# Last chunk's feed-forward first, bias rows in DRAM, held and split loads, two blocks normalized on chip, pooled score banks and order rules per stretch, in a fused layernorm, attention and feed-forward kernel

## The chip, the cores and the metric

One core of one Trainium2 chip. The metric is the device time of one execution in microseconds (us). Most executions of one kernel agree within 0.3%, but some runs of the kernel before come 4 to 6 us later with a lower mean granted clock of TensorE (0.987 to 0.991 for 0.996 to 1.0), so the clock of each run is looked at before its time is used.

The engines are called as the profile calls them: PE is TensorE (matrix products), PEld its weight loads, ACT is ScalarE, DVE is VectorE, POOL is GpSimd, SP is SyncE, which only issues transfers. An L with a number is a line of the kernel's own source, so the same work has another line number in the other kernel.

## The reference, cut to what matters

```python
# S = 2048 rows, D = 640, H = 32 heads of Dh = 20, F = 1536; all inputs bf16
def _A_ref(x, wq, wk, wv, wo):                    # one k and one v for all 32 heads
    q = (x @ wq).reshape(B, S, H, Dh).transpose(0, 2, 1, 3)
    k = x @ wk
    v = x @ wv
    scores = jnp.einsum("bhqd,bkd->bhqk", q, k) * (Dh ** -0.5)
    p = softmax(scores)
    o = jnp.einsum("bhqk,bkd->bhqd", p, v)
    return o.transpose(0, 2, 1, 3).reshape(B, S, H * Dh) @ wo

def _B_ref(x, w1, b1, w2, b2):
    h = x @ w1 + b1
    r = where(h > 0, h, 0)
    return (r * r) @ w2 + b2

xn = _layernorm(x)
return x + _A_ref(xn, wq, wk, wv, wo) + _B_ref(xn, w1, b1, w2, b2)
```

## The kernel before

The program is straight-line code whose order is decided when it is built. A list scheduler inside the kernel's source keeps a small model of the engines, and at every step puts the most urgent instruction that could start next onto its engine. On the chip each engine then runs its list in that order, whatever the real times are.

The attention has 32 blocks: 4 chunks of 512 queries by 8 groups of 4 heads. A block has 16 key tiles by 4 heads, so there are 2048 score tiles of 128 keys by 512 queries, each one bank of the on-chip accumulation memory (PSUM) wide. Most tiles become exponentials on ACT, two banks in one activation (a "step"). The others come in "sets" of four heads of one key tile: DVE turns four score banks into 16-bit patterns of approximate exponentials (line L972 of before), and three more passes on DVE or POOL refine them. PE makes the scores as row-tiled products (20 rows of one head each), and everything else as column-tiled products in groups of four. Changing between the two kinds costs PE time (0.32 us from the start of a run of scores to the next other product, and 0.105 back, as the prediction reads them below), and so score products are made in runs.

The score banks were two fixed pairs that take turns; three more banks served the sets and all other products:

```python
STATIC = True
SIDES = ((0, 1), (2, 3))
POOLED = tuple(bk for bk in range(NB) if not STATIC or bk not in sum(SIDES, ()))
...
def make_step():
    j = len(steps)
    if STATIC:
        banks = list(SIDES[j % 2])
        if any(bank_busy[bk] for bk in banks):
            return None
        return build_step(j, banks, 0.0)
```

A step is one activation of two banks:

```python
Op(f"ACT{j}", "ACT", 0.05 + 0.4267 * n, [lambda e: e.activation(
    out=PT[:, s0:s0 + n, :], in_=ps[:, b0:b0 + (n - 1) * db + 1:db, :],
    func=AF.Exp, bias=-EXP_SHIFT, scale=SCALE)], deps)      # PT is a ring of 20 slots
```

The feed-forward of each query chunk and its output projection were separate accumulations. The first wrote its result plus x to memory, and the second read it back. The bias b2 was one more product group per half row:

```python
def out_mats(st, half, cks, with_ffn):
    ...
    if with_ffn:
        for f in range(FT):                              # FT = 12
            mats.append((h2T[:, f, stl * 128:(stl + 1) * 128], w2_sb[:, f, cs]))
        mats.append((ones_bf[:, :], b2pad[:, cs]))       # the bias row
    ...
chain = []
for qc in range(QC):                                     # chunks in order 0, 1, 2, 3
    chain += [unit_FFN1(qc, f) for f in range(FT)] + [unit_FP(8 * qc + i) for i in range(8)]
```

All weight loads were issued at the start, behind the rows of x:

```python
l_w1 = load("w1", "SP", lambda e: e.dma_start(w1_sb[:], B_w1.rearrange(...)), 12.0)
...
l_wo = [load("wo", "SP", lambda e: e.dma_start(wo_c[:], A_wo.rearrange(...)), 14.0)]
```

Only the last of the 32 blocks was normalized on chip by transposes. For all others the sums went to memory, came back, were inverted, went to memory again and were read back as broadcast rows.

The softmax here doesn't subtract the row's maximum and nothing guards it: scores larger than these inputs give would overflow.

## Time and profile before

| | kernel before |
|---|---|
| time of a run, median | 727.65 us (727.4 to 728.07) |
| profiled span | 725.2 us |
| start until first exponential | 18.16 us |
| first exponential's start to last one's end (the phase) | 687.19 us |
| of it, ACT's floor: 744 steps at its pace of 0.904 us | 672.6 us |
| last exponential's end to the span's end (the tail) | 19.88 us |

The page, its slices, the costliest groups, the shares of the chain and the ends of the chain in time are shown in the prediction below. One more view of the kernel before: the busy time of each engine in stretches of 100 us, with PE's granted clock, the share of the transfer engines and the rate in GB/s.

```profile
core 0: us, PE busy (x) PEld busy (x) DVE busy (x) ACT busy (x) POOL busy (x), PEclk, DMA share, GB/s
100.00:200.00 100.00, 98.89 (x1377) 29.69 (x1381) 91.94 (x151) 100.00 (x111) 66.45 (x37) 1.00 0.17 45
200.00:300.00 100.00, 99.34 (x1331) 28.21 (x1327) 93.96 (x153) 100.00 (x111) 63.85 (x34) 1.00 0.15 41
```

ACT is busy in all 100 us of both stretches and PE in 99 of them.

### The profile page before, as it was taken

How to read it: one execution, taken by the hardware profiler on the slowest of the kernel's cores; microseconds unless marked ns; L12 is line 12 of the kernel's file. 1: busy time of each engine (PE TensorE's matmuls, PEld its weight loads, DVE VectorE, ACT ScalarE, POOL GpSimd, SP SyncE). 2: the span in 40 equal slices, each digit the busy share in tenths (PEclk: the TensorE clock that was granted, in tenths of full speed). 3: DMA queues.
4: the chain of work that ended last, by engine and by line, in shares of the span. 5: the costliest groups of instructions: out<-in, count | busy, mean ns of one | idle time of the engine just before them, and what ended most of it. 6: DMA issues, size and time to landing. Idle time of an engine off the chain costs nothing.

```text
span 725.2 us, 22939 instructions
## 1 busy us (share of the span) xinstructions
PE 710.5 (98%) x9952; PEld 220.5 (30%) x9952; DVE 647.5 (89%) x1136; ACT 691.6 (95%) x762; POOL 440.2 (61%) x269
## 2 busy tenths in 40 slices
PE   6999999999999999999999999999999999999997
PEld 3432222333322223223333222222332322223335
DVE  6769999899999999898799999898988999999985
ACT  4989999999999999999999999999999999999990
POOL 4625656767676656676655565656576576655751
PEclk9999999999999999999999999999999999999999
DMA  8500010211111012011211101122121111000211
GB/s 319 164 19 19 21 27 23 60 49 46 49 42 28 22 48 69 16 38 49 73 26 51 49 14 24 38 51 66 47 64 54 43 34 26 24 19 23 85 50 39
DMA packets 41015, 36.41 MB, mean 50 GB/s; under 512 B 15989, under 2 KB 35702, under 8 KB 40786
## 3 DMA queue, kind: packets, MB, share of 16 engines
q1 hardware_dynamic: 39970, 34.79, 17.1%
q8 instruction: 78, 1.28, 0.7%
q10 hardware_dynamic: 944, 0.15, 0.1%
q14 instruction: 23, 0.19, 0.1%
HBM read 20.24 MB, written 7.06 MB: 38 GB/s over the span
## 4 chain that ended last, share of the span: by engine, by line
ACT 69%; PE 29%; DMA 1%; DVE 1%; issue 0%; SPq 0%; DVEq 0%
ACT PT L807 69%; PE ps L283 28%; DMA x_sb<-in_A_x_dram 1%; PE ps L423 0%; DMA out_dram<-out_sb 0%; SPq L298 0%; PE ps L453 0%; PE ps L392 0%; DVE kT L467 0%; DVE big L353 0%; PE ps L411 0%; DVE out_sb L1204 0%; PE ps L481 0%; DVE kT L409 0%; DVE OR L343 0%
## 5 line engine op out<-in xcount | busy, mean ns | idle before, releaser
L807 ACT ACTIVATE PT<-ps 128x1024 bf16<-128x1024 f32 x744 | 682.6, 1179 | 8.5 <-PE ps L283 8.5
L972 DVE TENSOR_SCALAR tmore<-ps 128x512 uint16<-128x512 f32 x560 | 363.1, 682 | 38.8 <-PE ps L283 34.4
L990 POOL TENSOR_SCALAR x_sb<-tmore 128x2048 uint16<-128x2048 uint16 x136 | 257.0, 1899 | 159.3 <-DVE tmore L972 58.1
L283 PE MATMUL ps<-qT,kT 20*128 20x512 bf16 x2048 | 290.6, 384 | 3.9 <-ACT PT L807 2.2
L990 POOL TENSOR_SCALAR tmore<-tmore 128x2048 uint16<-128x2048 uint16 x85 | 161.1, 1903 | 87.2 <-DVE tmore L972 23.8
L283 PEld LDWEIGHTS ps<-qT,kT 20*128 20x128 bf16 x2048 | 72.3, 91 | 292.5 <-ACT PT L807 291.2
L283 PE MATMUL ps<-PT,vx 128*32 128x512 bf16 x1488 | 139.6, 386 | 0.3 <-ACT PT L807 0.3
L283 PE MATMUL ps<-x_sb,vxs 128*32 128x512 bf16 x1044 | 94.4, 382 | 0.0
L990 DVE TENSOR_SCALAR x_sb<-tmore 128x2048 uint16<-128x2048 uint16 x125 | 87.9, 727 | 0.1
L283 PE MATMUL ps<-xnT,w_sb 128*32 128x512 bf16 x960 | 76.8, 384 | 0.0
L283 PE MATMUL ps<-w_sb,big 128*32 128x320 bf16 x1536 | 73.7, 302 | 0.0
L283 PE MATMUL ps<-tmore,vxs 128*32 128x512 bf16 x636 | 59.2, 382 | 0.0
L283 PE MATMUL ps<-tmore,vx 128*32 128x512 bf16 x560 | 54.7, 382 | 0.1
L283 PEld LDWEIGHTS ps<-PT,vx 128*32 128x32 bf16 x1488 | 36.2, 94 | 61.0 <-issue 56.2
L990 DVE TENSOR_SCALAR tmore<-tmore 128x2048 uint16<-128x2048 uint16 x74 | 53.7, 742 | 0.1
L283 PEld LDWEIGHTS ps<-w_sb,big 128*32 128x32 bf16 x1536 | 32.6, 95 | 29.0 <-issue 20.9
L561 DVE TENSOR_SCALAR hT_tmp<-ps,b1col 128x512 bf16<-128x512 f32 x48 | 35.7, 744 | 5.2 <-PE ps L283 4.7
L283 PE MATMUL ps<-xnT,wq_sb 128*32 128x512 bf16 (+1 forms) x480 | 33.6, 356 | 0.0
L283 PEld LDWEIGHTS ps<-x_sb,vxs 128*32 128x32 bf16 x1044 | 24.6, 95 | 22.2 <-issue 14.3
L283 PE MATMUL ps<-wo_c,OC 128*32 128x320 bf16 x640 | 30.8, 301 | 0.0
L569 DVE TENSOR_TENSOR big<-hT_tmp 128x512 bf16<-128x512 bf16 x48 | 26.5, 561 | 0.0
L283 PEld LDWEIGHTS ps<-xnT,w_sb 128*32 128x32 bf16 x960 | 17.4, 94 | 26.0 <-issue 22.7
(81 smaller groups left out, 278.0 us busy)
## 6 DMA issues: line engine op xcount, KB each, us to landing
w_sb<-in_B_w_dram SPq DMA_DIRECT2D x2, 1920.0 KB, 15.3
fpd<-fpw SPq DMA_DIRECT2D x24, 160.0 KB, 1.9
fpr<-fpd SPq DMA_DIRECT2D x24, 160.0 KB, 2.4
big<-OR SPq DMA_DIRECT2D x74, 40.0 KB
big<-drs SPq DMA_DIRECT2D x74, 40.0 KB
xr<-in_A_x_dram SPq DMA_DIRECT2D x32, 80.0 KB, 2.1
out_dram<-out_sb SPq DMA_DIRECT2D x16, 160.0 KB, 1.8
qT<-QCr SPq DMA_DIRECT2D x108, 20.0 KB
```

The lines of the kernel that those rows point to most:

```text
L283: return lambda e: e.matmul(out_, l, r, start=start, stop=stop, tile_position=tp)
L561: o = Op(f"RL{qc}_{f}", "DVE", 0.66, [lambda e: e.tensor_scalar(out=hT_tmp[:, k % 2, :], in0=ps[:, bk, :], scalar1=b1col[:, f:f + 1], scal ...
L569: q = op(f"SQ{qc}_{f}", "DVE", 0.34, lambda e: e.tensor_tensor(out=h2T[:, f, :], in0=hT_tmp[:, k % 2, :], in1=hT_tmp[:, k % 2, :], op=ALU. ...
L807: return Op(f"ACT{st_['j']}", "ACT", 0.05 + 0.4267 * n, [lambda e: e.activation(out=PT[:, s0:s0 + n, :], in_=ps[:, b0:b0 + (n - 1) * db + ...
L972: d1 = op(f"D1_{n}_{i}", "DVE", 0.60, lambda e: e.tensor_scalar(out=L[:, cs].bitcast(U16), in0=ps[:, bank, :], scalar1=XA, scalar2=XB, op0 ...
L990: p = op(f"P{j}_{n}", eng, 0.60 if eng == "DVE" else 1.86, lambda e, T=T, j=j, two=two: e.tensor_scalar(out=T.bitcast(U16), in0=L.bitcast( ...
```

## The change

Its intent: cut the two ends of the program, in which ACT has nothing to do; take products away from PE (bias groups, runs of scores); and let the scheduler weave the rest tighter, with score banks taken from a common pool and its settings changed per 10 us of ACT's time. The core of the diff, with cuts marked:

```diff
-STATIC = True
+STATIC = False
-POOLED = tuple(bk for bk in range(NB) if not STATIC or bk not in sum(SIDES, ()))
+POOLED = tuple(range(NB))
-NL = 4
-NT = 8
+NL = 5
+NT = 9
+HOLD = dict(wq="TE2", b1="TE5", w1=("TE4", "TE6", "TE8", "TE10"), w2=("RL3_2", ...), wo=("RL3_10", "FE24"), b2="VE8", ...)
+STG = 10.0
+RULES = {3: {'PVA': 2.1, 'PVD': 2.1, 'R3': 1, 'PP': 0.9},
+         ... # some fifty stretches
+         69: {'R3': 0, 'JIT': 1.1}}
 ...
-        l_w1 = load("w1", "SP", lambda e: e.dma_start(w1_sb[:], B_w1.rearrange(...)), 12.0)
+        l_w1 = [load(f"w1{k}", "SP", lambda e, k=k: ..., 8.0, [HOLD["w1"][k]]) for k in range(4)]
 ...
-                mats.append((ones_bf[:, :], b2pad[:, cs]))
+        # x + b2 is made in memory: 16 broadcast copies of b2, then 8 accumulating transfers of x
+            o = op(f"XB{st}", "POOL", 1.25, lambda e, r0=r0, r1=r1: e.dma_start(xbd[r0:r1, :], A_x[0][r0:r1, :], accum_op=ALU.add, ...), ...)
 ...
-        for qc in range(QC):
-            chain += [unit_FFN1(qc, f) for f in range(FT)] + [unit_FP(8 * qc + i) for i in range(8)]
+        for qc in [QC - 1] + list(range(QC - 1)):
+            chain += [(unit_FFN1(qc, f), 0.0) for f in range(FT)]
+            chain += [(unit_FP(8 * qc + i), 0.0) if qc == QC - 1 else (unit_OUT(8 * qc + i), G * (qc + 1) + OUT0) for i in range(8)]
 ...
-            if len(ok) >= 3 + R3:
+            if len(ok) >= 3 + par("R3"):       # three neighbouring free banks: one step of three
 ...
-            if b == NBLK - 1:
+            if b >= NBLK - 2:                   # normalized on chip
 ...
-                consider("PE", 1, make_pv(b, x), ("pv", b, k))
+                consider("PE", par("PVA"), make_pv(b, x), ("pv", b, k))
+            if tail_begun():
+                for o, p, x, bk in tail_ops():
+                    consider("PE", p, o, ("tail", o, x, bk))
```

The name `par` looks a setting up in the rules of the current stretch, and else in the defaults.

## The prediction

> **What bounds the kernel now.** I read the page's busy times first, then its slices, the chain that ended last, the costliest groups, and last the order in time of the start and of the end. The page of the kernel before:
>
> ```profile
> span 725.2 us, 22939 instructions
> PE 710.5 (98%) x9952; PEld 220.5 (30%) x9952; DVE 647.5 (89%) x1136; ACT 691.6 (95%) x762; POOL 440.2 (61%) x269
> ACT  4989999999999999999999999999999999999990
> ...
> PEclk9999999999999999999999999999999999999999
> ...
> L807 ACT ACTIVATE PT<-ps 128x1024 bf16<-128x1024 f32 x744 | 682.6, 1179 | 8.5 <-PE ps L283 8.5
> L972 DVE TENSOR_SCALAR tmore<-ps 128x512 uint16<-128x512 f32 x560 | 363.1, 682 | 38.8 <-PE ps L283 34.4
> ```
>
> Two engines are full at once. ACT does nothing but exponentials (744 of two score banks) from the second slice on, and has an empty last slice; PE is almost never idle, at full clock. DVE, which makes 560 of the 2048 score tiles into exponentials by its own route, has a tenth to spare. The chain is shared between ACT and PE by turns:
>
> ```profile
> ACT 69%; PE 29%; DMA 1%; DVE 1%; issue 0%; SPq 0%; DVEq 0%
> ```
>
> A share does not say how tight either is, so I took it apart in the trace's records.
> ACT: of the 743 steps from one exponential's start to the next, 479 are 0.904 to 0.909 us and none is shorter, so 0.904 is its pace. 744 x 0.904 = 672.6 us. From the first start (18.16) to the last end (705.34) are 687.2, so 14.6 us are lost: 4.6 in three long waits, the rest in many short ones.
> PE: a run of score products is followed by the next run of other products 0.32 us after its start, and the run after it starts 0.105 after the last other product has taken its turn, so a run of scores costs 0.43 us however many it holds (2 to 4). Four column-tiled products of 512 columns cost 0.2155, of 320 columns 0.136 (48 of them, twelve groups, start 1.63 us apart from the next kind). The built program's listing after the first score product has 735 runs of scores, 1305 groups of 512 and 584 of 320: 316 + 281 + 79, with 7 of transposes and small ones 683.7 us. From the first score (17.73) to the last product's end (720.4) are 702.7, so PE loses 19 us, 2.7%.
> So neither engine alone can be relieved with profit; both must shrink, or the stretches outside the common phase must. There are two such stretches. The start, in order of time:
>
> ```profile
> 2.17 4.61 DMA x_sb<-in_A_x_dram
> ...
> 14.72 0.31 PE ps L453 x5
> 15.03 2.16 issue
> 17.19 0.61 PE ps L423 x2
> 17.79 0.38 PE ps L283 x4
> 18.18 1.01 ACT PT L807
> ```
>
> The fourth row of x lands only 4.61 us after its issue, and at 15.03 PE stands 2.16 us with nothing that it waited for, while the transfers of the weights hold the queues (0.91 busy share, 374 GB/s in that stretch). The end, in order of time:
>
> ```profile
> 709.75 0.11 PEld L283 LDWEIGHTS ps<-b2pad,ones_bf 128*32 128x32 bf16 x4
> ...
> 710.66 0.71 DVE L866 STREAM_TRANSPOSE OR<-ps 128x512 f32<-128x512 f32 x1
> ...
> 713.77 5.33 PE L283 MATMUL ps<-wo_c,OC 128*32 128x320 bf16 x152
> ...
> 718.93 1.12 PE L283 MATMUL ps<-wo,QCr 128*32 128x320 bf16 x28
> ...
> 722.10 0.89 DVE L1204 TENSOR_TENSOR out_sb<-ps,w_sb 128x320 bf16<-128x320 f32 x2 [0.33 <-DMA out_dram<-out_sb]
> ```
>
> After the last exponential (705.34) PE still has 16.4 us of products: the last chunk's second feed-forward product with its bias rows (to 713.7), then all of its output projection. 19.9 us of the span lie behind the exponentials.
>
> **What the Trainium skill says.** "ScalarE: Activation LUTs", section "What ACT_TABLE_LOAD costs": an activation takes 0.833 ns an element plus a fixed part, whatever the function. The trace agrees in the slope as far as one size can show it: 1024 x 0.833 = 853 ns, which leaves 51 ns fixed in a pace of 904. So one of three banks should cost 0.904 + 0.427 = 1.331 us, an estimate from the page and this pace, as the trace has none. "TensorE: Matmul & The Clock Gate", section "Back-to-back issue gap": N/2.4 + 2.5 ns when warm, 215.8 and 135.8 for 512 and 320; the trace's 215.5 and 136 agree, and four column tiles share one such turn. "PSUM — Partial Sum Buffer", section "Specifications (TRN2)": eight banks, and GpSimdE neither reads nor writes them; the trace has no POOL group with a bank in it, and in the changed tail POOL adds only what ACT has copied out. "DMA: Bandwidth & Descriptors", section "SWDGE vs HWDGE vs iDMA": accumulating transfers can only be issued from GpSimd; no run of the kernel before has one.
>
> **The change, part by part.**
> 1. Last chunk's feed-forward first. Its eight partial results go to memory early and return in one load; the other three chunks do the second feed-forward product and the output projection in one accumulation, so 24 writes, 24 reads and 24 evacuations vanish. The tail keeps the output projection alone, and most of that may start under the last block's exponentials. By the listing PE has 6.3 us of products after the last score instead of 16.4.
> 2. Bias rows: x + b2 is made in memory by eight accumulating transfers, so the 32 bias groups of 320 go: 32 x 0.136 = 4.4 us of PE. With them the last block but one leaves the chain of memory round trips: 8 groups more of that weight, 8 fewer of the other.
> 3. Pooled banks and rules. Score steps now take any free neighbours of seven banks, three at a time 50 times: 665 x 0.904 + 50 x 1.331 = 667.7 us against 672.6, 4.9 less on ACT. Runs of scores fall from 735 to 714: 21 x 0.43 = 9.0 us. Two more sets go to DVE and POOL (142 against 140), fills fall from 18 groups to 3. PE after the first score: 307 + 279 + 75 + 5.4 = 666.8, 16.9 less.
> 4. DVE: 8 tiles more (5.5 us) and 18 more passes (217 against 199, 0.73 each, 13.1), 34 evacuations of 0.485 fewer (16.5), 1.4 for the second normalization on chip, four copies of q to ACT (1.1): about +2.4, to 650. POOL: 209 passes for 221 at 1.9 us, 23 less, plus the issue of nine transfers.
> 5. Loads held and split, x on two queues, q copied by ACT into its own banks: in the start. I give the row of x 1 to 1.5 us, the stand at 15.03 about 2, the shorter wait for k about 0.5: first exponential at 14.3 instead of 18.16, 3.9 us.
>
> **The sum.** Tail from the last exponential: 0.7 to the last product and its latency; the normalization of the last block, by the end before, 710.66 to 713.12, 2.5; eight closing groups and the eighth half's four, 2.1 with their latency; evacuation 0.8; output 2.2, as before from 722.99 to 725.2. Together 8.3 instead of 19.9: 11.6 us. By ACT: 14.3 + 667.7 + 8.3 = 690.3 plus losses. By PE: 13.9 + 666.8 + 4.8 (from its end to the span's end, as before) = 685.5 plus losses. With the losses of before, 14.6 and 19, they give 704.9 and 704.5; with half, 697.6 and 695. Pooled banks let scores be made ahead, so I take the losses a little under before's: span 701.5. Run times lie 2.4 us over the profiled span (727.65 to 725.2): 704 us, 3.2% less.
>
> **Rivals.**
> A: only the two ends count. The rules shift work, but two engines that are 97 to 98% full cannot be woven tighter, and losses grow as fast as work shrinks: the phase stays 687 us long. Then 14.3 + 687.2 + 8.3 + 2.4 = 712. For it: 687.2 came out with a tuned order already. Against: 16.9 us of PE's work really go.
> B: DVE or POOL takes the bound. DVE has 650 us in about 680, 94% in some stretches before (93.96 in 200 to 300), and each bank now also waits for DVE's evacuation before the pool has it again. It would show as scores waiting for DVE: 708 to 716.
> C: The new round trip through memory comes late. The x + b2 rows pass through three transfers and POOL's own issue, and a late row stalls DVE in its fixed order. Each output unit has a row, so a few 2 us stalls would be seen: 706 to 712. For it: nothing of the kind is in the trace, so its latency is unknown. Against: each row is asked for three units ahead, and the queues are 17% busy.
> D: Everything fits as the author's rules intend, losses of 6 us: 699.
>
> **Range and chances.** The ends give 15.5 us that hardly depend on the weaving; 727.65 - 15.5 = 712 is the bad case A, and 2% faster is 713.1. The sum with small losses is 697. Range 696 to 712. Faster by over 2%: 0.92; within 2%: 0.07; slower by over 2%: 0.01, for a stall in an order that is fixed when the program is built.
>
> **What would show it.** The first exponential starts at about 14.3 and the stand of PE before it is gone. 50 activations of three banks step by about 1.33. From first start to last end are 672 to 680. The last end is 8 to 9 before the span's end, and no feed-forward product lies in it. PE stays busy at 98%, DVE near 650 of busy time. Wrong would be: the phase still near 687 (A), waits of scores for DVE above some us (B), evacuations or sums waiting for transfers of the summed rows (C), a tail over 12 us, or a clock below full.

## The result, and the profile after

The changed kernel takes 705.51 us (median of 4 runs, 705.35 to 705.72, every clock 0.999 or 1.0), the kernel before on the same occasion 727.86 us (4 runs, 727.4 to 732.43). The ratio is 0.968, with an interval of 0.964 to 0.972. Ratios here are the mean time of one kernel's fast runs over the mean of the other's fast runs of the same rounds, so they are not quite the ratio of the medians that are quoted, which is 0.969. The prediction was 704 us with a range of 696 to 712.

The page of the changed kernel, with the rows that answer to those shown of before:

```profile
span 703.6 us, 22608 instructions
...
PE 695.0 (99%) x9780; PEld 216.0 (31%) x9781; DVE 645.9 (92%) x1125; ACT 687.5 (98%) x739; POOL 427.3 (61%) x268
ACT  6899999999999999999999999999999999999995
...
ACT 95%; PE 4%; DMA 1%; DVE 0%; SPq 0%; issue 0%; DVEq 0%
...
L910 ACT ACTIVATE PT<-ps 128x1024 bf16<-128x1024 f32 (+1 forms) x715 | 677.1, 1219 | 3.8 <-PE ps L367 3.8
L1083 DVE TENSOR_SCALAR tmore<-ps 128x512 uint16<-128x512 f32 x568 | 367.4, 683 | 31.7 <-PE ps L367 28.2
```

ACT's last slice is now half full, where it had nothing before: the tail is shorter. ACT has 715 exponentials for 744. The chain, 69% ACT and 29% PE before, is now 95% ACT. The last column of the two groups gives what the engine waited for: the exponentials waited 3.8 us for products (8.5 before).

The chain in order of time (start, duration, and what it was) begins and ends so:

```profile
2.46 5.39 DMA x_sb<-in_A_x_dram
...
7.88 0.83 ACT OC L421 x2
8.71 1.18 ACT xnT L477 x2
...
14.94 0.32 PE ps L367 x2
...
32.44 661.79 ACT PT L910 x699
...
694.27 3.90 PE ps L367 x104
...
698.18 0.89 PE ps L367 x20
...
699.10 1.28 DVE out_sb L1164 x3
```

From 32.44 on ACT is never released by anything but itself for 661.79 us. Before, PE stood 2.16 us at 15.03; here the first scores come at 14.87 without a stand. The chain ends with 3.90 and 0.89 us of PE's output projection. PE's last product ends 5.1 us after the last exponential (695.14 to 700.26), where it had 15.1 us of feed-forward and projection before (705.34 to 720.4).

Where the 21.6 us between the two profiled spans come from, taken from the records of the exponentials in the two traces:

| us | before | after | difference |
|---|---|---|---|
| start until first exponential | 18.16 | 15.30 | -2.86 |
| ACT's floor | 672.6 | 667.7 | -4.9 |
| ACT's waits over 0.25 us | 5.2 | 3.0 | -2.2 |
| ACT's other losses | 9.4 | 9.1 | -0.3 |
| tail | 19.88 | 8.50 | -11.38 |

A wait counts here as a step's time over the pace (the 4.6 us in three waits of the prediction are ACT's idle time in the same three). The floor is the steps times the pace: 744 x 0.904 before, 665 x 0.904 + 50 x 1.331 after. Both paces are read from the trace; 1.331 is the median of the steps of three banks.

### The profile page after: what moved, and what is told of

It is laid out like the page before. It is cut to its first block, busy times and chain, and to the rows that moved or that the text cites. A ratio compares the mean times of both kernels' runs of the same rounds, so it can differ in the third digit from the quotient of the medians.

```text
span 703.6 us, 22608 instructions
## 1 busy us (share of the span) xinstructions
PE 695.0 (99%) x9780; PEld 216.0 (31%) x9781; DVE 645.9 (92%) x1125; ACT 687.5 (98%) x739; POOL 427.3 (61%) x268
## 4 chain that ended last, share of the span: by engine, by line
ACT 95%; PE 4%; DMA 1%; DVE 0%; SPq 0%; issue 0%; DVEq 0%
ACT PT L910 94%; PE ps L367 3%; DMA x_sb<-in_A_x_dram 1%; PE ps L540 1%; ACT xnT L477 0%; ACT OC L421 0%; DVE out_sb L1164 0%; PE ps L568 0%; SPq L384 0%; ACT OC L422 0%; SPq L391 0%; PE ps L510 0%; PE ps L496 0%; DVEq L227 0%; DVE PT L1164 0%
## 5 line engine op out<-in xcount | busy, mean ns | idle before, releaser
L910 ACT ACTIVATE PT<-ps 128x1024 bf16<-128x1024 f32 (+1 forms) x715 | 677.1, 1219 | 3.8 <-PE ps L367 3.8
L1083 DVE TENSOR_SCALAR tmore<-ps 128x512 uint16<-128x512 f32 x568 | 367.4, 683 | 31.7 <-PE ps L367 28.2
L1101 POOL TENSOR_SCALAR tmore<-tmore 128x2048 uint16<-128x2048 uint16 x109 | 206.4, 1900 | 171.1 <-PE ps L367 62.3
L367 PE MATMUL ps<-qT,kT 20*128 20x512 bf16 x2048 | 281.7, 384 | 1.9 <-ACT PT L910 0.8
L1101 POOL TENSOR_SCALAR x_sb<-tmore 128x2048 uint16<-128x2048 uint16 x100 | 189.3, 1902 | 79.4 <-DVE x_sb L1101 24.2
L1101 DVE TENSOR_SCALAR x_sb<-tmore 128x2048 uint16<-128x2048 uint16 x135 | 96.1, 745 | 0.1
L367 PE MATMUL ps<-x_sb,vxs 128*32 128x512 bf16 x940 | 83.2, 382 | 0.0
L367 PE MATMUL ps<-tmore,vxs 128*32 128x512 bf16 x764 | 69.6, 382 | 0.0
L1101 DVE TENSOR_SCALAR tmore<-tmore 128x2048 uint16<-128x2048 uint16 x82 | 61.5, 770 | 0.1
L367 PEld LDWEIGHTS ps<-x_sb,vxs 128*32 128x32 bf16 x940 | 21.3, 95 | 19.9 <-issue 13.4
L367 PEld LDWEIGHTS ps<-tmore,vxs 128*32 128x32 bf16 x764 | 18.1, 95 | 16.4 <-issue 11.5
```

The costliest lines, as they stand in the source:

```text
L367: return lambda e: e.matmul(out_, l, r, start=start, stop=stop, tile_position=tp)
L910: return Op(f"ACT{st_['j']}", "ACT", 0.05 + 0.4267 * n, [lambda e: e.activation(out=PT[:, s0:s0 + n, :], in_=ps[:, b0:b0 + (n - 1) * db + ...
L1083: d1 = op(f"D1_{n}_{i}", "DVE", 0.60, lambda e: e.tensor_scalar(out=L[:, cs].bitcast(U16), in0=ps[:, bank, :], scalar1=XA, scalar2=XB, op0 ...
L1101: p = op(f"P{j}_{n}", eng, 0.60 if eng == "DVE" else 1.86, lambda e, T=T, j=j, two=two: e.tensor_scalar(out=T.bitcast(U16), in0=L.bitcast( ...
```

## The experiments

The prediction said that neither ACT nor PE could be relieved alone with profit. In the expectations of f_peplus, f_peminus and f_actminus the theory M still says so: both engines are full and lock each other; R1 there is that PE alone sets the time, R2 that ACT alone does. None of the three fits all of those runs, and from b_ffnfirst on M (later also H2) is another theory: ACT leads the common phase and PE follows with a little room, and the time is ACT's floor plus a small loss plus the two ends. Its main rival (R1, later H1) is that PE's sum of work sets the time. For a_nohold and b_hold the theories are about the start. Twelve kernels were run. The table gives all of them, read from the traces in the same way; "floor" is ACT's steps times their measured pace, and "PE" is the work of PE from the first score on, counted in the built program's listing with the durations that the prediction gives (for f_peplus and f_peminus the changed kernel's with the groups added or left out and the runs of scores counted again).

| kernel | median us | span | first exp. | phase | floor | tail | PE |
|---|---|---|---|---|---|---|---|
| before | 727.65 | 725.2 | 18.16 | 687.19 | 672.6 | 19.88 | 683.7 |
| changed | 705.51 | 703.6 | 15.30 | 679.84 | 667.7 | 8.50 | 666.8 |
| f_peplus | 719.0 | 716.8 | 15.15 | 693.16 | 667.7 | 8.51 | 684.2 |
| f_peminus | 706.18 | 703.9 | 15.59 | 679.82 | 667.7 | 8.50 | 645.1 |
| f_actminus | 697.03 | 695.0 | 15.06 | 670.73 | 647.8 | 9.23 | 666.8 |
| a_nohold | 717.89 | 714.9 | 16.84 | 689.55 | 667.7 | 8.51 | 666.8 |
| b_ffnfirst | 727.38 | 725.0 | 17.90 | 695.29 | 679.8 | 11.78 | 685.0 |
| b_hold | 726.72 | 726.5 | 18.18 | 688.43 | 672.6 | 19.87 | 683.7 |
| a_norules | 716.07 | 714.5 | 15.61 | 687.00 | 671.9 | 11.85 | 670.0 |
| a_static | 716.9 (one run) | 715.2 | 14.95 | 688.34 | 672.6 | 11.87 | 676.9 |
| f_ffnminus | 728.11 | 725.8 | 18.55 | 695.46 | 679.8 | 11.79 | 662.0 |
| b_ffntuned | 725.44 | 723.0 | 16.82 | 691.56 | 676.2 | 14.58 | 682.4 |
| a_swap | 705.49 | 703.4 | 15.11 | 679.82 | 667.7 | 8.50 | 666.8 |
| a_no3 | 718.76 | 716.9 | 14.89 | 692.37 | 672.6 | 9.66 | 677.1 |

Names that begin with f keep the order of instructions exactly and change only the amount of work in some of them; a starts from the changed kernel and b from the kernel before, and these are woven anew by the scheduler where the edit touches it. The three occasions of four kernels each had seven runs of the kernel before beside them: 726.1 to 733.4 us, 726.3 to 732.7 and 726.0 to 733.2. The changed kernel itself was not run again on them; a_swap, the same order but for one instruction, gave 705.37 to 705.99 on the last, so times on the three occasions may be set against 705.5.

### More work for PE in the same order

```diff
 # changed kernel; n is the number of groups in one accumulation of a half row
+                z = 4 if n >= FT and k == 1 else 0
-                ... col4(lambda j: l[:, 32 * j:32 * j + 32], r, 320, kk, ...)
+                ... col4(...) + [m for _ in range(z) for m in col4(lambda j: zeros32[:, :], r, 320, 1, False, 32, bank)]
```

The 128 groups more have weights of zero and add zero to the sums: 128 x 0.136 = 17.4 us of PE.

> The changed kernel in its own fixed order, with 128 groups of 320-column products by a zero weight added inside the 32 accumulations of the second feed-forward product: 128 x 0.136 = 17.4 us more of PE, nothing else moved (the result is unchanged). Theory M, both engines are full and lock each other: PE's idle of some 18 us is made of pieces between runs that it cannot use, so most of it shows: 713 to 721. Rival R1, PE alone is the limit: 705.5 + 17.4 = 723. Rival R2, ACT alone is the limit and PE has room: 705 to 708.

Measured: correct, 719.0 us (718.88 to 719.56), 13.5 more than the changed kernel. M's range holds it, R1 and R2 miss. The phase grew by 13.3 us, so PE took 4.1 of the 17.4 us without any effect: that is the room it had where these groups were put. ACT's loss over its floor is 25.5 us (12.1 in the changed kernel), most of the added part in some 30 waits of 0.3 to 0.6 us.

### Less work for PE in the same order

```diff
+                z = n >= FT and 1 <= k <= 4
+                ... [lambda e: None] if z else col4(...)       # wrong result on purpose
```

> The same fixed order with 4 of the 12 groups left out of each of those 32 accumulations: 17.4 us less of PE (wrong result on purpose). M: ACT keeps its floor of 667.7 and only its short waits shrink, 12.1 us are lost now, so 698 to 703. R1: 688. R2: 705.

Measured: 706.18 us (705.04 to 707.32), no gain at all. M had expected some, and missed; R2 hit. The pages of the two f kernels, f_peminus first:

```profile
span 703.9 us, 21585 instructions
...
PE 680.1 (97%) x9269; PEld 205.1 (29%) x9269; DVE 645.8 (92%) x1125; ACT 687.4 (98%) x739; POOL 426.6 (61%) x268
...
ACT 95%; PE 4%; DMA 1%; DVE 0%; SPq 0%; DVEq 0%; issue 0%
```

```profile
span 716.8 us, 23633 instructions
...
PE 708.6 (99%) x10293; PEld 228.9 (32%) x10293; DVE 646.9 (90%) x1125; ACT 693.6 (97%) x739; POOL 426.4 (59%) x268
...
PE 66%; ACT 31%; DVE 1%; DMA 1%; issue 0%; SPq 0%; DVEq 0%
```

The groups alone are 17.4 us. Ten runs of scores merge as well (704 for 714, counted in the trace), which makes 21.7 us less by the prediction's costs; PE is busy 14.9 us less and the span is the same. Its busy share hardly tells: 97% with that work gone, 99% as it was and 99% with 17.4 us more. The shares of the chain tell in these three: 95% ACT where PE has room, 66% PE where PE is short.

### Less work for ACT in the same order

```diff
-  e.activation(out=PT[:, s0:s0 + n, :], in_=ps[:, b0:...:db, :], func=AF.Exp, ...)
+  e.activation(out=PT[:, s0:s0 + n, 0:496], in_=ps[:, b0:...:db, 0:496], func=AF.Exp, ...)
```

The 16 columns left out hold ones. It was meant to be wrong, but the result passed within the tolerance of the comparison.

> The same fixed order with 496 of 512 columns in every exponential of ACT (wrong result on purpose; the other columns hold ones): 1480 tiles x 16 x 0.833 ns = 19.7 us less of ACT. M: PE keeps its 667 us of work with its switches, so the time falls by 2 to 8: 697 to 703. R1: 705. R2: 686.

Measured: 697.03 us (696.05 to 697.86), at the lower edge of M's range; both rivals miss. The pace of a step of two fell to 0.877 us and of a step of three to 1.291, so the floor to 665 x 0.877 + 50 x 1.291 = 647.8 us, 19.9 less. The phase shortened by 9.1. The rest was lost to waits for PE, and the chain shows who leads now:

```profile
span 695.0 us, 22609 instructions
...
PE 94%; ACT 4%; DVE 2%; DMA 0%; issue 0%; DVEq 0%
```

So relief of ACT alone gains about half of it, and then PE is the bound: by this run PE's room is about 9 us, by f_peplus about 4. Relief of PE alone gains nothing.

### All weight loads at the start

```diff
-        l_w1 = [load(..., 8.0, [HOLD["w1"][k]]) for k in range(4)]      # likewise wq, b1, w2, wo
+        l_w1 = [load(..., 8.0, []) for k in range(4)]
```

The order on PE, ACT, DVE and POOL is unchanged.

> The changed kernel with the loads of all weights issued at the start as before, though still split; the order on PE, ACT, DVE and POOL is the same. If the stand of 2.16 us before the first score came from the queues being full of weights, it comes back: first exponential at about 17.5 instead of 15.3 and 707 to 708. Rival: the stand belonged to the old order (its two extra warming products, its bank of q), and nothing changes: 705.5. A third outcome, a late row of x as well, would be 709 or more.

Measured: 707.78, 716.81, 718.98 and 719.83 us. The clock was 0.999 in the first of these and 0.980 to 0.982 in the others. From the run of 716.81 us, first PE's row in the order of time (start, duration, engine, line, operation, tiles, count, and in brackets the idle time before it with what ended it):

```profile
15.81 0.39 PE L510 MATMUL ps<-hT_tmp,OR 128*128 128x512 bf16 x1 [1.82 <-issue]
```

The clock row of its page, in tenths of full speed per slice of 17.9 us:

```profile
PEclk9589999999999999999999999999999999999999
```

And two stretches of 5 us with busy times of PE, PEld, DVE, ACT and POOL, the granted clock, transfer share and rate:

```profile
20.00:25.00 5.00, 5.00 (x50) 1.48 (x49) 2.83 (x13) 3.40 (x5) 2.18 (x4) 0.50 1.07 359
...
30.00:35.00 5.00, 5.00 (x36) 0.81 (x38) 2.43 (x12) 3.07 (x3) 2.61 (x4) 0.50 0.03 7
```

The stand of the kernel before is back: 1.82 us in which PE waits for nothing that the profile names, just before the first scores. The first exponential comes 1.5 us later. And then PE's clock falls to half and stays there until after 40 us, in stretches where PE is counted busy all the time. ACT loses 9.6 us more in the first 100 us than in the changed kernel (13.5 for 3.9). In the one run where the clock did not fall, which has no trace, the loads at the start cost 2.3 us (707.78 for 705.5); where it did, 11 to 14. So the expected 707 to 708 holds for one run of four, the first exponential missed (16.84 for 17.5), and none of the outcomes named the clock. The Trainium skill's page "TensorE: Matmul & The Clock Gate", section "What's actually happening", lets the clock fall to half after at least one idle window of about 3.4 us and rise after one busy window of the same length. The fall agrees in kind, but the stand seen here is 1.82 us, and half clock lasted over 20 us of continuous busy time.

What the stand waits for is not named by the profile. The records of transfers give a hint: one packet of 16 KB of the queue that brings instructions comes at 14.65 us in the kernel before, and PE stands from 15.03 to 17.19; here it comes at 13.38 and PE stands from 13.99 to 15.81; in the changed kernel it comes at 11.34, and nothing stands. In all six traces in which this packet comes between 13.4 and 14.7 us, PE stands 1.8 to 2.8 us. In the other eight, the changed kernel among them, it comes between 10.9 and 11.5 us, and PE has no such stand. PE's own rows in the traces (products, weight loads and a few others) say more. The queue brings 78 such packets in the kernel before, whose page has 9952 products and 9952 weight loads: about 255 rows to a packet. In all six traces PE stops after the same number of its rows, 449, and goes on 1.3 to 1.9 us after the packet's end; and in the changed kernel the next packets start when PE has passed 478, 712 and 969 rows, shortly after 449, 449 + 256 and 449 + 512. So the stand lies where one block of PE's instructions ends, and lasts until the next one has come. That the weights make this packet late is shown only as far as a_nohold goes: with them at the start it starts at 13.38 us for 11.34. No run moved a block's end to test the reading.

### The last chunk's feed-forward first, alone, in the kernel before

```diff
-for qc in range(QC):
+for qc in [QC - 1] + list(range(QC - 1)):
     chain += [unit_FFN1(qc, f) for f in range(FT)] + [unit_FP(8 * qc + i) for i in range(8)]
 # the eight partial results of the last chunk go to memory like the others and return in one load; FFN0 = 0.3
```

> The kernel before with one part of the change alone: the last chunk's feed-forward comes first in the chain and its partial results go through memory; static score banks, bias rows, loads and everything else as before. By the built program's listing PE has 685.0 us of work after the first score product (683.7 before) and 7.2 us of products after the last score instead of 16.4. Theory M (ACT leads the common phase, so only the work of PE behind the last exponential is paid): the tail falls by the 9.2 us that leave it, 716 to 721 us, with the phase still 686 to 689 long. Rival R1 (PE's sum sets the time, as my prediction's second chain had it): the same or 1 to 2 us longer, 727 to 730, because the products that leave the tail fill the phase. Rival R2 (between: the full phase takes the products in at the price of about half of them): 722 to 725.

Measured: 727.38 us (726.32 to 731.97), no gain. M's expectation missed, R1's number hit. But the trace says why: the tail did fall, from 19.88 to 11.78 us, and the phase grew by the same 8.1 us, because ACT has 752 steps for 744 (8 x 0.904 = 7.2 us). The scheduler, which has more products to place before the end, found room for four sets fewer and left 16 tiles more to ACT. The 752 could have been read from the listing before the run; the expectation of M used the tail alone.

That leaves two readings: PE was short on the chip (H1), or ACT still led and the scheduler's choice made it longer (H2). The next experiment tells them apart.

### The same order with less work for PE

```diff
 # b_ffnfirst
+                z = n > FT and 1 <= k <= 4
+                ... [lambda e: None] if z else col4(...)       # wrong result on purpose
```

> The kernel before with the last chunk's feed-forward first, in exactly the order of instructions in which it ran before at 727.4 us, with four of the twelve groups left out of each of the 32 second feed-forward products (wrong on purpose). PE has 23 us less to do (662.0 after the first score for 685.0, some score runs merge), none of it behind the last exponential; ACT still has its 752 steps. Theory H2 (ACT leads here too; the tail's gain went because the order that the scheduler wove gives ACT 8 steps more than before, and PE's room only decided that when the program was built): 724 to 727, the phase between first and last exponential 693 to 695 (695.3 with all groups). Rival H1 (PE itself is the bound of the phase on the chip): 706 to 716, with the phase 10 us or more shorter. Between them, 718 to 723, both count.

Measured: 728.11 us (727.39 to 733.31). The phase is 695.46 us, with all groups it was 695.29. The total is a little over H2's range (in the profiled run the start was 0.65 us later); H1 misses by 12 us or more.

```profile
span 725.8 us, 21762 instructions
...
PE 698.7 (96%) x9367; PEld 207.8 (29%) x9368; DVE 647.6 (89%) x1109; ACT 699.0 (96%) x770; POOL 438.2 (60%) x268
...
ACT 91%; PE 6%; DVE 1%; DMA 1%; issue 0%; SPq 0%; DVEq 0%
```

The page shows PE at 96% for 98%, and the chain at ACT. 23 us of PE's work gone, and nothing gained. In this order of the old design, too, ACT leads on the chip. The share of the chain misleads here: b_ffnfirst has 21% PE in its chain and f_ffnminus 6%, and that share was worth no time. PE counts when the program is built: what it has to do decides how many sets the scheduler can place, and each set that is not placed gives ACT four tiles, two steps of 0.904 us.

### Other settings for the whole program

```diff
 # b_ffnfirst
-JIT = 0.65      NOPEN = 2    DRATE = 0.95    BEHIND = 0.12    PEND = NBLK - 3.0
+JIT = 0.9       NOPEN = 3    DRATE = 0.85    BEHIND = -0.3    PEND = NBLK - 2.0
```

It was chosen from the listings of several sets of settings, for the smallest sum of ACT's steps and PE's work behind the last score.

> The kernel before with the last chunk's feed-forward first, woven with other settings of the scheduler, one set for the whole program (three open sets for two, scores made earlier, sets made with less slack, the other products pressed sooner). By the listing ACT has 748 steps (752 in the first version, 744 in the kernel before), PE 682.4 us (685.0, 683.7) and 7.0 us behind the last score (7.2, 16.4). H2 (ACT's steps and the tail set the time): 4 x 0.904 + 0.2 = 3.8 less than 727.4: 722.5 to 724.5. H1 (PE's sum): 2.6 less, 724 to 726. Rival (the settings of before were tuned, others bring waits that no sum shows): 727 or more.

Measured: 725.44 us (724.78 to 727.71). H2's range misses by 1 us, H1's holds it, the third is out. The trace splits it: the phase is 3.7 us shorter, as the four steps fewer ask, and the start is 1.1 us shorter, but the tail is 2.8 us longer, though the listing has 0.2 us less work there. In order of time, near the end:

```profile
713.37 0.64 DVE L904 TENSOR_TENSOR OC<-big 48x512 bf16<-48x512 f32 x1
...
714.06 2.68 PE L283 MATMUL ps<-wo_c,OC 128*32 128x320 bf16 x52 [2.95 <-DVE OC L904]
```

PE stands 2.95 us for the last normalization rows of the block before the last. They came by the round trip through memory, but that is not what was late: the last packets of these reads (2048 bytes each) end at 705.9 us, 7.5 us before. DVE took the rows up only at 713.37, because in its fixed order this pass stands behind the normalization of the last block. The changed kernel normalizes both blocks on chip, and its projection needs no such rows; the sum of listed work does not see this wait.

### Weight loads held, in the kernel before

```diff
+        hold = te_op[3]
-        l_w1 = load("w1", "SP", ..., 12.0)                  # likewise b1, w2, b2, wo, wo7
+        l_w1 = load("w1", "SP", ..., 12.0, [hold])
```

> The kernel before with its weight loads held until the fourth transpose group of the start is done; the order of instructions on PE, ACT, DVE and POOL is the same as before. Theory M (the stand of 2.16 us that PE had at 15.03, waiting for nothing the profile names, comes from the weight loads that fill the queues): the stand is gone, first exponential at about 16.0 instead of 18.16, time 724 to 726.5. Rival R1 (the stand has another cause, such as the order itself): stand still there, first exponential at 18 and 727 to 729. Rival R2 (the held loads now come late for the first feed-forward products or the transposed weights): the start is earlier but a wait for a transfer of 1 us or more appears after it, 726 to 730.

Measured: 726.72 us (726.06 to 728.34), which is not told apart from the 728.4 of its occasion (ratio 0.997, interval 0.993 to 1.002). M missed: the first exponential came at 18.18, as R1 has it, though R1's time missed by 0.3. PE's row in the order of time:

```profile
16.61 0.99 PE L424 MATMUL ps<-hT_tmp,ones_bf 128*128 128x512 bf16 x2 [2.15 <-issue]
```

Two stretches, with the columns as in the stretches of a_nohold:

```profile
10.00:15.00 5.00, 3.95 (x163) 3.22 (x155) 4.40 (x19) 2.97 (x8) 1.85 (x3) 1.00 1.11 345
...
17.50:20.00 2.50, 2.50 (x13) 0.93 (x12) 1.16 (x6) 1.82 (x2) 0.06 (x1) 0.50 0.93 376
```

The stand is still there, 2.15 us, and half clock after it. But the run does not test the cause: the held loads were issued from 12.88 us on, before the stand, and the other transfers kept the queues full from 10 to 15 us (share 1.11). It shows only that a release point of this kind, in the middle of the rows' own loads, buys nothing.

### No rules

```diff
-RULES = {3: {...}, ..., 69: {...}}
+RULES = {}
```

> The changed kernel with its table of rules per stretch emptied, so that the scheduler weaves every stretch by the same defaults. By the listing: ACT's exponentials need 671.9 us (667.7 with rules; 26 steps of three banks for 50), 140 sets on the other engines, PE 670.0 us after the first score (666.8), 9.7 us of products after the last score (6.3). Theory M (ACT's floor plus the tail): 705.5 + 4.2 + 3.4 = 713, 711 to 715. Rival R1 (PE's sum): 705.5 + 3.2 = 708.7, 707 to 710. Rival R2 (rules are there to avoid waits, which the sums do not show): long waits of ACT of 3 us or more appear besides, 716 to 722.

Measured: 716.07 us (715.51 to 716.31), 10.6 more than the changed kernel. M's range (711 to 715) misses by 1 us; R1 misses by far. The span grew by 10.8: 4.2 in the floor, 3.3 in the tail, 2.9 in ACT's losses (one wait of 2.1 us at 455 us, one of 0.6 at 350, the rest in small ones), 0.3 at the start. R2 has the number at its edge but not the size: it named waits of 3 us or more besides the sums, and all the added waits together are 2.9. ACT's waits for products in the exponentials (total, times, longest):

```profile
ACT PT L860 <- PE ps L317: 5.7, 5, 1.9
```

### No rules and fixed pairs

```diff
-STATIC = False
+STATIC = True
+RULES = {}
```

> The changed kernel without rules and with the score banks as in the kernel before: two fixed pairs by turns, no step of three banks. By the listing: ACT 672.6 us (671.9 without rules alone), PE 676.9 (670.0), 10.1 us of products after the last score (9.7). To be read against the changed kernel without rules, on the same chip. Theory M (ACT leads): 0.7 + 0.4 = 1.1 us more than without rules, at most 2 more for waits on the fixed pairs, as the kernel before had them. Rival R1 (PE's sum): 6.9 us more. Rival R2 (pooling is what lets scores be made ahead, so ACT's losses double without it from 12 us): 10 us or more above it.

Measured: one run at clock 1.0 took 716.9 us; three others took 726.64, 726.8 and 741.62 at clocks of 0.984, 0.984 and 0.96. The clean run is 0.8 us above the median of the kernel without rules, near M's 1.1, and far from 6.9 (R1) and 10 (R2). There is one clean run only, and no trace of the others, so how the clock came to fall in them stays open. By this run the pool of banks with the defaults gains under 1 us by itself. PE has 6.9 us more to do here than without rules, and that is not seen in the time.

### Rules and pool, but no steps of three

```diff
-            if len(ok) >= 3 + par("R3"):
+            if False:
```

> The changed kernel with its rules and pooled banks, but no step of three banks (the scheduler weaves it anew with the same rules). By the listing ACT has 744 steps of two, 672.6 us (667.7), because it gets 8 tiles more with two sets fewer on the other engines (3.6 us) and the three-bank steps' saving is gone (50 x 0.025 = 1.3); PE 677.1 us (666.8), 7.4 us behind the last score (6.3). ACT leads: 705.5 + 4.9 + 1.1 = 711.5, 710.5 to 713. PE's sum: 705.5 + 10.3 = 715.8, 714 to 718. Rival (the rules were tuned for one order and hurt any other): more than the 716.1 without rules.

Measured: 718.76 us (718.66 to 719.55), more than without any rules. Both sums missed, and the rival hit. ACT's floor and the tail grew by 4.9 and 1.2 as listed, but its losses went from 12.1 to 19.8. ACT's waits for products (total, times, longest):

```profile
ACT PT L910 <- PE ps L367: 10.5, 9, 3.1
```

And the end of the longest in order of time:

```profile
595.40 0.39 PE L367 MATMUL ps<-PT,vx 128*32 128x512 bf16 x4
...
595.84 1.94 ACT L910 ACTIVATE PT<-ps 128x1024 bf16<-128x1024 f32 x2 [3.15 <-PE ps L367]
```

The scores that this step needs are older than the wait. What ends it is a product that reads exponentials of the ring PT, and none such starts between 584.07 us and 595.40, while PE makes feed-forward products and products of the sets. By then ACT has written 1248 tiles and PE has used 1228: the ring of 20 slots was full, and ACT had nowhere to write. The table of rules has 'PVA': 2.1 for one stretch there (1 by default), which puts ACT's products behind the others; that this rule did it was not tested. The rules are settings fitted to one order. In another order the same numbers hurt.

### One instruction moved in the changed kernel

```diff
+        mv_ = next(o for o in order_all if o.name == "S5a")      # ACT's first pass over the sixth row block
+        order_all.remove(mv_)
+        order_all.insert(1 + order_all.index(te_op[1]), mv_)      # behind the evacuations of the first two
```

> The changed kernel in its own order but for one instruction: ACT's first pass over the sixth row of x, for which it waited 1.64 us while the transposes of the first two rows lay finished, comes behind the two evacuations of those. Theory (ACT's place in its order delays the start): first exponential 0.5 to 0.8 us earlier than 15.3, and all after it: 704.6 to 705.1. Rival (k and v of the first chunk wait for the later rows anyway): within 0.2 us of 705.5, or a little over it because the sixth row's statistics come later.

Measured: 705.49 us (705.37 to 705.99); the rival hit. ACT in order of time, the changed kernel first and then the moved one:

```profile
7.88 0.74 ACT L421 ACTIVATE OC<-x_sb 128x640 bf16<-128x640 bf16 x1 [1.64 <-DMA x_sb<-in_A_x_dram]
...
8.61 1.28 ACT L477 ACTIVATE xnT<-ps 128x640 bf16<-128x640 bf16 x2
...
11.54 1.30 ACT L477 ACTIVATE xnT<-ps 128x640 bf16<-128x640 bf16 x2
```

```profile
7.61 1.30 ACT L477 ACTIVATE xnT<-ps 128x640 bf16<-128x640 bf16 x2 [1.37 <-PE ps L475]
8.80 0.74 ACT L421 ACTIVATE OC<-x_sb 128x640 bf16<-128x640 bf16 x1
...
11.37 1.28 ACT L477 ACTIVATE xnT<-ps 128x640 bf16<-128x640 bf16 x2
```

The first two evacuations came 1.0 us earlier and the next two only 0.17. Between them ACT still makes all its passes over the rows that come later, from 8.80 to 11.46 without a gap: the wait was moved out of the way, the work was not. Moving those passes behind the fourth evacuation would be the next try; it was not run.

## Why the prediction was right

The time and the class (faster by over 2%) held, and most terms of the sum did. One step of its reasoning, the second chain, did not.

- **The ends.** The tail was put at 8.3 us and is 8.50. The terms that it was made of can be seen in the chain. The feed-forward product that filled it is gone, and the last but one block needs no rows from memory; in b_ffntuned, where it does, the late pass over them costs 2.95 us. The 16.4 us that the prediction puts after the last exponential of the kernel before are the listing's work after the last score; the trace has 15.1 after the exponential.
- **The first exponential** was put at 14.3 us and came at 15.30. The stand of 2.16 us is gone as predicted, and a_nohold brings it back by undoing the held loads. The term that was too large is the gain on the rows of x: the fifth and sixth row blocks landed 5.39 us after their issue, and ACT waited 1.64 us for them in front of evacuations that were ready. In a_swap this wait is gone from its place and the first exponential comes 0.2 us earlier, less than the spread of the three f kernels that share one start (15.06 to 15.59); the passes of ACT over later rows hold the place.
- **ACT's floor** was worked out from the page "ScalarE: Activation LUTs" and the pace: 667.7 us, 1.331 for a step of three. The 50 steps of three have a median of 1.331, so the term held to the digit. Most of its 4.9 us comes from the two more sets (eight tiles, 3.6 us), only 1.3 from the steps of three.
- **Losses** were taken as 11.2 us and are 12.1: most stretches of the middle lose about 1.4 us in 100, in both kernels and also in f_peminus and f_ffnminus. What these small losses are stays open; more room for PE does not change them. The prediction took the losses under before's because pooled banks let scores be made ahead. That reason is not what the runs show: with the pool but no rules (a_norules) they are 15.1, and only with the rules 12.1.
- **The sum.** 14.3 + 667.7 + 8.3 + 11.2 = 701.5 was the span; 15.30 + 667.7 + 8.50 + 12.1 = 703.6 is. The runs lie 1.7 to 2.0 us over their own spans. The 2.4 set the median of three runs of the kernel before against the span of another, which took 727.06, 1.9 over it; this slip made up for a part of the terms that came out larger.
- **The second chain of the prediction was wrong.** "So neither engine alone can be relieved with profit; both must shrink": f_actminus gains 8.5 us with ACT alone relieved, f_peminus and f_ffnminus gain nothing with 22 and 23 us less for PE. The sum by PE (685.5 plus losses) agreed with the sum by ACT because PE's idle time of 19 us was counted as a loss of the same kind, and that they agreed within half a microsecond was luck. In the two orders that were tested it was slack; the kernel before in its own order was not tested so. The 16.9 us less for PE were needed all the same: f_peplus puts 17.4 us back in the changed order and loses 13.5. How they paid is argued from this and from b_ffnfirst: they gave the scheduler room, so that the products of the tail could move into the phase without taking sets away. b_ffnfirst shows the move without that room: 8.1 us off the tail, 8.1 us onto the phase.
- **Rival A** (only the ends count, 712) is refuted: the phase shortened by 7.35 us. It comes close to what a_norules and a_static do (687.0 and 688.3 us of phase). The ends with the structural parts, without rules or pool, bring 10.1 us of span (725.2 to 715.2, a_static), the pool 0.7 (to 714.5, a_norules) and the rules, with the steps of three that they allow, 10.8 (to 703.6); by a_no3 these two cannot be parted. No run takes out the bias rows, the split of the loads or the second block's normalization alone, so what each of them is worth is not shown.
- **Rival B** (DVE or POOL bounds): DVE was put at 650 us and has 645.9; PE's named waits for DVE are 0.6 us in all. **Rival C** (late rows of x + b2): the accumulating transfers landed 5.8 us after their issue and the rows 2.4 us after theirs, and no wait of an evacuation for one of them is named. **Rival D** (losses of 6 us) did not come.

Not in the prediction: the clock. Seven of the 21 runs of the kernel before beside the experiments have a clock under 0.992 and take 731 us or more, while no run of the changed kernel has, nor any of the sixteen of f_peplus, f_peminus, f_actminus and a_swap, which keep its order and its held loads. Held loads alone are not enough: a_static has them too, and three of its four runs had clocks of 0.96 to 0.984. The run of 732.43, whose clock is not on record, is in the quoted ratio of 0.968; without it the medians are 705.51 and 727.65, 3.0% less.

## What to carry to other kernels

Two engines that are both busy 98% need not be equally bound, even where the second has only 4 to 9 us of room in 680, as here: change the work of one in an unchanged order, up and down, and see which of them moves the time. In a program whose order is woven at build time, an engine with slack on the chip can still cost time through what the scheduler leaves to the others, so count the bound engine's instructions in the listing before believing that a shorter tail is a gain. Settings tuned to one order belong to that order; after any structural edit they have to be tuned again or dropped.

## What the Trainium skill lacked or had wrong

- "ScalarE: Activation LUTs", section "What ACT_TABLE_LOAD costs": an activation with immediate scale and bias has a fixed 186 ns of which back-to-back ones hide 93. Here 93 ns would remain; the pace of 0.904 us for 1024 columns and 1.331 for 1536 leaves 51. The slope agrees: (1.331 - 0.904) / 512 is 0.834 ns a column. The section does not say in which memory its operands lay, and the skill does have the figure elsewhere: "Perfetto Trace Analysis", section "Optimizing Scalar/DVE Operations", gives about 93 ns for ScalarE on SBUF and about 51 on PSUM, which these activations read.
- "TensorE: Matmul & The Clock Gate", section "What's actually happening": the clock fell to half after stands of 1.82 (a_nohold), 2.15 (b_hold) and 2.81 us (f_ffnminus), shorter than the idle window of about 3.4 us, and in a_nohold it stayed at 0.50 from 20 to 40 us with PE counted busy throughout, where one busy window should have raised it. In the other two it was back by 20 to 25 us. Three stands of the same kind (2.16 us in the kernel before, 2.70 in b_ffnfirst, 1.89 in b_ffntuned) were followed by full clock.
- "Runtime: NRT & Kernel Launch", section "Instruction fetch mechanics", says that an engine's instructions come in blocks of 16 KiB by its own transfers and calls the cost of a block's end mostly hidden. It does not say what full queues do to it: in the six traces where such a packet came late (13.4 to 14.7 us) PE stood 1.8 to 2.8 us without a named wait, after 449 of its rows each time.
- "TensorEngine Tiling (Array Packing)", section "Key Properties", says that changing the tiling mode drains the engine, without a figure: here the next products start 0.32 us after a run of row-tiled scores began, and the scores 0.105 us after the last turn of the others.
- No page gives the time of an accumulating transfer: 640 KB landed 5.8 us after the issue (median of eight).
